# A recurrent attention block with dense layers on one core: the output projection with its weight as the stationary side, dense layers on rows of both network layers at once, and a lag of 4 steps instead of 6

## The chip, the core and the metric

The kernel runs on one core of a Trainium2 chip. The time is device microseconds of that core, as the median of several executions. The engines are called PE (TensorE), DVE (VectorE), ACT (ScalarE), POOL (GpSimd) and SP (the engine that only issues transfers here). The time before is 1830.54 us (3 runs, 1828.23 to 1834.61).

## The reference, cut to what matters

Two network layers with the same weights run one after the other. Each is an attention part that walks over the 2048 rows in 64 segments of 32 rows, then a dense part. The attention of a segment sees 8 memory rows and its 32 rows. The first 8 rows of its projected output are the memory of the next segment, so the 64 steps of one layer are a chain.

```python
def _A_ref(x, mem0, Wq, Wk, Wv, Wo, seg_len):        # 32 heads of 128, Dm = 512
    mem = mem0
    for s in range(n_seg):                            # 64 segments of 32 rows
        h = jnp.concatenate([mem, x[:, s*32:(s+1)*32, :]], axis=1)   # 40 rows
        q, k, v = (jnp.einsum('btd,dhe->bhte', h, W) for W in (Wq, Wk, Wv))
        p = _softmax(jnp.where(mask, q @ k^T * scale, -1e9))
        o = jnp.einsum('bhte,hed->btd', p @ v, Wo)
        mem = o[:, :M, :]                             # the chain
        outs.append(o[:, M:, :])
    return jnp.concatenate(outs, axis=1)
# ... cut: _B_ref(x) = relu(x @ w1) @ w2, with 1376 hidden columns
x = x + _A_ref(_layernorm(x), ...);  x = x + _B_ref(_layernorm(x), ...)
x = x + _A_ref(_layernorm(x), ...);  x = x + _B_ref(_layernorm(x), ...)
```

## The kernel before

The kernel works on both network layers in one step: layer one on segment k, layer two on segment k - DELTA (DELTA is the lag, 6). So there are 64 + 6 = 70 steps: 58 with both layers, and 6 with one layer at each end. The instruction order on each engine is found on the host before compilation, by a planner that tries 60 orders, partly at random from a seed, with assumed costs and keeps the best; its constants are no measurements. The order that it chose is then fixed: each engine executes its own queue in that order.

The projection has the attention's output as its stationary side (64 columns: 16 rows and both memories of layer one and two, and 32 rows of layer two) and Wo as the moving side (512 columns). Its result has rows on partitions. The next step's queries need the memory with the 512 features on partitions. So the memory is copied out, turned by small matmuls, and copied again: this is called the hand-over below.

```python
    def project(k, act, seg):
        ...
        for p in range(4):
            def mm(p=p):
                for hh in range(4):
                    for u in range(2):
                        h = 8 * p + 4 * u + hh
                        nc.tensor.matmul(wo[64 * u:64 * u + 64, :], lhsT=OT[:, h, HS:2 * L], rhs=Wo_sb[:, h, :],
                                         start=(p == 0 and hh == 0), stop=(p == 3 and hh == 3),
                                         tile_position=(0, 64 * u))
        ...                      # the hand-over:
            for half, eng in ((0, ACT), (1, DVE)):       # wm[:, half] <- wo[:, half], 128x256 each
                ...
            def tr(cols):                                # turn: mt <- wm against selm
                ...
            def ev():                                    # HTn memory columns <- mt (DVE)
                ...
        for a in act:                                    # row adds: x rows += wo, two per layer (DVE)
            ...
                plan.op(DVE, t_dve(512), add, r=[wo, x], w=[("x", g, c)])
        if 0 in act:                                     # OXb <- first 16 rows of layer one (POOL)
            ...

    def project_late(g):         # once in four steps: those 16 rows of four segments, 32 matmuls of 512
        ...                      # columns, a copy, a spread against selx, one add
```

The other 16 rows of each layer-one segment do not fit into the 64 columns; they wait for `project_late`. The dense part (`finish_group`) runs per layer on 128 rows, the rows of four segments. The values of each step are needed in a second place for layer one: transfers from on-chip memory to on-chip memory put them there (`place_values`: one transfer per half, which waits for all four value copies).

Of the kernel before, what the change touches and what calls it, by code (L numbers as in the profile page):

```python
# [18 lines left out]
DELTA = 6  # L19
# [9 lines left out]
PASSES = 60  # L29

# [53 lines left out]
class Op:  # L84
    __slots__ = ("eng", "cost", "fn", "preds", "succs", "bufs", "new", "given", "ready", "start", "end", "wait",
                 "after", "seq", "tile", "lag", "mode", "more")


class Plan:
# [7 lines left out]
    def op(self, eng, cost, fn, r=(), w=(), tile=WHOLE, lag=None, more=0.0):  # L97
        o = Op()
        o.eng, o.cost, o.fn, o.succs, o.seq, o.tile = eng, cost, fn, [], len(self.ops), tile
# [28 lines left out]
    def forward(self, prio, look, stay):  # L128
# [3 lines left out]

        for pool in self.pools:
            pool.reset()
# [6 lines left out]
        for o in self.ops:  # L141
            if not o.wait:
                cand[o.eng].append(o)
        count, tile = 0, WHOLE
        while count < len(self.ops):
            best = None
            for e in range(5):
                lo = None
                for o in cand[e]:
                    t = max(o.ready, free[e])  # L150
                    for pool, bufs in o.new:
                        t = max(t, pool.when(bufs))
                    o.start = t
                    if lo is None or t < lo:
                        lo = t
                if lo is not None and lo < 1e9 and (best is None or lo < best[0]):
                    best = (lo, e)
            assert best is not None, "no operation can be planned"
            lo, e = best
            o = min((c for c in cand[e] if c.start <= lo + look),  # L160
                    key=lambda c: (prio[c.seq] - (stay if e == PE and c.tile in (tile, EITHER) else 0.0), c.seq))
# [20 lines left out]
            for s in o.succs:  # L182
                s.ready = max(s.ready, seen)
                s.wait -= 1
                if not s.wait:
                    cand[s.eng].append(s)
# [47 lines left out]
    def order(self):  # L234
# [13 lines left out]
        rnd, best, look, stay = Random(1), None, 0.05, 0.5  # L248
        for n in range(PASSES):
# [5 lines left out]
            if best is None or total < best[0]:  # L255
                best = (total, [(o.start, o.seq, o.mode) for o in self.ops], [(b, b.i) for b in self.bufs], look, stay)
                base = late
# [3 lines left out]
        for _, seq, mode in best[1]:  # L261
            self.ops[seq].mode = mode
        return [self.ops[seq] for _, seq, _ in sorted(best[1])]
# [3 lines left out]
def kernel(  # L267
# [35 lines left out]

# [3 lines left out]
    LK = (0, L - HS)  # L307
    plan = Plan()
# [17 lines left out]
    p_x = Pool([sb(f"xg{i}", [128, Dm], F32) for i in range(4)], True)  # L326
    p_b = ring("bf512", 1, [128, Dm])
    x0 = p_x.buf()
    xb0 = p_b.buf()
    xb0_t = p_b.tiles[0]  # L330
# [40 lines left out]

    selm = sb("selm", [128, 2 * M])
    selx = sb("selx", [128, 128])

# [8 lines left out]
    def make_mask():  # L383
        nc.gpsimd.memset(maskb[:], 0.0)
        for g2 in range(2):
            blk = maskb[64 * g2:64 * g2 + SEG, 0, 0:HS]
            select(blk, ALU.is_ge, NEG, 0, -1, 1)
            select(blk, ALU.is_ge, NEG, HS - 1, 0, -1)
            blk = maskb[64 * g2:64 * g2 + SEG, 0, HS:SEG]
            select(blk, ALU.is_ge, NEG, -HS, -1, 1)  # L390
            select(blk, ALU.is_ge, 0.0, -HS, 0, 1)
# [3 lines left out]

    def make_selm():
        nc.gpsimd.memset(selm[:], 0.0)
        for u in range(2):
            select(selm[64 * u:64 * u + 64, :], ALU.not_equal, 1.0, -HS, -1, 1)

    def make_selx():
        nc.gpsimd.memset(selx[:], 0.0)
        for u in range(2):
            for c in range(GS):
                select(selx[64 * u:64 * u + 64, SEG * c + HS:SEG * (c + 1)], ALU.not_equal, 1.0, -HS * c, -1, 1)
# [11 lines left out]
    OXb = sb("OXb", [128, H, GS * HS])  # L417
    wxs = sb("wxs", [128, Dm])
    wm = sb("wm", [128, Dm])
# [7 lines left out]
    p_xn = [ring("xnA", 2, [128, NC4, 128], BF, True), ring("xnB", 1, [128, NC4, 128], BF, True)]  # L427
# [4 lines left out]
    def prepare():  # L432
# [10 lines left out]
        def zero_rest():  # L443
            nc.vector.memset(OT[:], 0.0)
            for t in (*Pt, *p_PT.tiles, V0, vw):
                nc.vector.memset(t[:], 0.0)

        def get_x():
            nc.scalar.dma_start(out=xb0_t[:], in_=A_x[0, 0:128, :])

        def get_memory():
            nc.scalar.dma_start(out=wm[0:M, :], in_=A_mem0[0, :, :])
# [3 lines left out]
        def turn():  # L456
            for c4 in range(NC4):
                nc.tensor.transpose(tp[:, :].bitcast(BF)[:, c4 * M:(c4 + 1) * M],
                                    wm[0:M, c4 * 128:(c4 + 1) * 128], ident[0:M, 0:M])
# [8 lines left out]
        columns = [("HTm", i) for i in range(2)] + [("HTx", i, a, c) for i in range(2) for a, c in ((0, 0), (0, HS), (1, X1))]  # L468
        plan.op(ACT, 0.45, get_x, w=[xb0])
        plan.op(ACT, 0.45, get_memory, w=[("wm", 0), ("wm", 1)])  # L470
# [3 lines left out]
        plan.op(DVE, 9.0, zero_rest, w=["zero PT"] + [("vw", p) for p in range(4)] + [("V0l", b) for b in range(2)] + [("OT", j) for j in range(8)] + [("P", p, b) for p in range(4) for b in range(2)])  # L474
        plan.op(POOL, 0.6, make_ident, w=["ident"])
        plan.op(POOL, 3.3, make_mask, w=["mask"])
        plan.op(POOL, 0.6, make_selm, w=["selm"])
        plan.op(POOL, 2.0, make_selx, w=["selx"])
        plan.op(PE, 0.2, turn, r=[("wm", 0), ("wm", 1), "ident", "memory"], w=[tp])
# [9 lines left out]
    def layernorm(x, rows, pool):  # L489

        ln, xn, xnT, tp = p_ln.buf(), p_b.buf(), pool.buf(), b_fill.buf()

        def stats():
            nc.vector.bn_stats(out=ln[:, 0:6], in_=x[:, :])

        def aggr():
            nc.vector.bn_aggr(out=ln[:, 6:8], in_=ln[:, 0:6])

        def eps():
            nc.vector.tensor_scalar_add(out=ln[:, 8:9], in0=ln[:, 7:8], scalar1=LN_EPS)  # L500

        def power():
            nc.gpsimd.tensor_tensor(out=ln[:, 8:9], in0=ln[:, 8:9], in1=mhalf_t[:], op=ALU.pow)

        def norm():
            nc.vector.tensor_scalar(out=xn[:, :], in0=x[:, :], scalar1=ln[:, 6:7], scalar2=ln[:, 8:9],
                                    op0=ALU.subtract, op1=ALU.mult)

        def turn(cols):
            for c4 in range(NC4):  # L510
                for u in range(0, 128, cols):
                    nc.tensor.transpose(tp[u:u + cols, :].bitcast(BF)[:, c4 * 128:(c4 + 1) * 128],
                                        xn[:, c4 * 128 + u:c4 * 128 + u + cols], ident[:], tile_position=(0, u))

        def keep():
            nc.scalar.copy(out=xnT[:, :, :].rearrange("p c t -> p (c t)"), in_=tp[:, :].bitcast(BF)[:, 0:512])
# [5 lines left out]
        plan.op(DVE, 0.50, norm, r=[x, ln, *rows], w=[xn])  # L522
        plan.op(PE, 0.23, turn, r=[xn, "ident"], w=[tp], tile=EITHER)
        plan.op(ACT, t_act(512), keep, r=[tp], w=[xnT])
        return xnT

    def dense_layer(x, rows):
        xnT = layernorm(x, rows, p_xm)
        hT = p_h.buf()
        for fb in range((NFC + 3) // 4):  # L530
# [14 lines left out]
            def relu(hp=hp, f0=fcs[0], n=nfull):  # L545
                nc.scalar.activation(out=hT[:, f0:f0 + n, :].rearrange("p f t -> p (f t)"), in_=hp[:, 0:n * 128],
                                     func=ACTF.Relu)

            def relu_last(hp=hp, n=nfull):
                nc.scalar.activation(out=hT[0:F_LAST, NFC - 1, :], in_=hp[0:F_LAST, n * 128:(n + 1) * 128],  # L550
                                     func=ACTF.Relu)

            plan.op(ACT, t_act(128 * nfull), relu, r=[hp], w=[hT, (hT, fb)])
            if nfull < len(fcs):
                plan.op(ACT, t_act(128), relu_last, r=[hp], w=[hT, (hT, fb)])
# [11 lines left out]
        def add():  # L567
            nc.vector.tensor_tensor(out=x[:, :], in0=x[:, :], in1=yp[:, :], op=ALU.add)

        plan.op(DVE, t_dve(512), add, r=[yp, x], w=rows)  # L570

    x_tiles, xnT_tiles = {}, {}

    def rows_of(g):
        return [("x", g, c) for c in range(GS)]

    def load_group(g):
        x, xb = (x0, xb0) if g == 0 else (p_x.buf(), p_b.buf())
# [4 lines left out]
        def widen():  # L583
            nc.vector.tensor_copy(out=x[:, :], in_=xb[:, :])

        if g > 0:
            plan.op(SP, 0.6, load, r=["loaded"], w=[xb, x])
        plan.available(xb0, 3.5)
        plan.op(DVE, 0.36, widen, r=[xb], w=[x, *rows_of(g)])
        x_tiles[g] = x  # L590
        xnT_tiles[(0, g)] = layernorm(x, rows_of(g), p_xn[0])

    def finish_group(a, g):
        x, rows = x_tiles[g], rows_of(g)
        dense_layer(x, rows)
        if a == 0:
            xnT_tiles[(1, g)] = layernorm(x, rows, p_xn[1])
            return
        assert out.dtype == BF
        ob = p_b.buf()  # L600

        def narrow():
            nc.scalar.copy(out=ob[:, :], in_=x[:, :])

        def store():
            nc.sync.dma_start(out=out[0, 128 * g:128 * (g + 1), :], in_=ob[:, :])

        plan.op(ACT, t_act(512), narrow, r=[x, *rows], w=[ob])
        plan.op(SP, 0.6, store, r=[ob])
# [13 lines left out]
    def t_copy(eng, n, rate=1):  # L623
        return t_act(n) if eng == ACT else t_dve(n, rate)

    def prep_x(k):
# [4 lines left out]
        for a in act:  # L631
            g, c = divmod(seg[a], GS)
# [383 lines left out]
```

## Time and profile before

| | before |
|---|---|
| median of 3 runs | 1830.54 us |
| profiled span | 1826.9 us |
| mean granted PE clock (share of full speed) | 0.986 |
| end of the first projection (start of its last matmul) | 58.5 us |
| a step with both layers (mean of 58) | 26.38 us |
| a step with one layer | 18 to 22 us |

The step times are differences between the starts of the last projection matmuls of successive steps, read from the trace.

First the page of the kernel before: the span, then busy time, share of the span and number of instructions of each engine (PEld is the weight load of a matmul), and the chain that ended last, by engine and by line.

```profile
span 1826.9 us, 84214 instructions
...
PE 1680.4 (92%) x37465; PEld 1293.2 (71%) x37465; DVE 1301.0 (71%) x3147; ACT 901.9 (49%) x2146; POOL 424.8 (23%) x1177
...
PE 75%; DVE 9%; DMA 7%; ACT 5%; issue 2%; SPq 1%; POOL 0%; POOLq 0%; ACTq 0%; DVEq 0%
```

The next view is the timeline of the kernel before around one hand-over; columns are start and duration in us, engine, line, operation, output<-inputs, shape, count and, in brackets, idle time of the engine before and what ended it.

```profile
923.67 1.06 PE L867 MATMUL st_123<-Wo_sb,OT 128*64 128x512 bf16 x8
...
924.53 1.06 PE L487 MATMUL fill_125<-w_sb,hT_117 128*64 128x512 bf16 x8
924.76 0.37 ACT L619 CAST wm<-st_123 128x256 bf16<-128x256 f32 x1 [1.44 <-PE st_123 L867]
925.16 0.43 DVE L621 CAST wm<-st_123 128x256 bf16<-128x256 f32 x1 [1.63 <-ACT wm L619]
...
925.39 0.48 PE L487 MATMUL work_122<-selm,wm 128*64 128x16 bf16 x8
925.62 0.68 DVE L906 TENSOR_TENSOR xg_68<-xg_68,st_123 16x512 f32<-16x512 f32 x1
...
926.33 0.23 DVE L890 CAST HT_79<-work_122 128x64 bf16<-128x64 f32 x1
926.39 1.03 PE L667 MATMUL fill_124<-Wv_sb,XG 128*64 128x512 bf16 x8
...
927.35 0.75 PE L719 MATMUL work_119<-HT_79,Wk_sb 128*128 128x80 bf16 x16
```

The last eight projection matmuls start at 923.67. ACT's copy, DVE's copy after it, the turn, a row add that got in between, and the memory copy into HT_79 take until 926.56. In the meantime PE runs dense matmuls and values of later rows (fill). The first query/key matmul starts at 927.35. On the mean of the both-layer steps, the last projection matmul starts 2.67 us before the next step's first query or key matmul, and the rest of the step (first query to last projection) takes 23.69 us.

Two groups of that hand-over from the table of groups (busy us, mean ns, idle before, releaser) show that DVE's half of the copy always follows ACT's (69 times of 69, 0.03 us after its end):

```profile
L621 DVE CAST wm<-st_123 128x256 bf16<-128x256 f32 x69 | 29.3, 425 | 105.9 <-ACT wm L619 105.9
L619 ACT CAST wm<-st_123 128x256 bf16<-128x256 f32 x69 | 25.7, 372 | 61.9 <-PE st_123 L867 61.9
```

The last view before the change is of the value tile V_87 in the stretch with both layers (241 to 1693 us): who waited for the transfers into it (us in all, times). PEld and PE together waited 41.1 us.

```profile
who waited for it (us, times):
  PEld L840: 10.8, 9
  PE work_120 L840: 9.3, 9
  PE work_118 L840: 9.1, 8
  PE work_121 L840: 4.5, 8
  PE work_122 L840: 3.8, 6
  PE work_119 L840: 3.6, 7
```

### The profile page before, as it was taken

To read this page: it belongs to the slowest core of one execution; us is meant where nothing else is said; L and a number is where in the kernel's file an instruction comes from. 1 tells how busy PE (TensorE), PEld (TensorE's weight loads), DVE (VectorE), ACT (ScalarE), POOL (GpSimd) and SP (SyncE) were. 2 spreads that over 40 slices of the span, in tenths; PEclk is the share of its full clock that TensorE was granted. 3 is DMA by queue.
4 is the path that set the end of the run, shared out by engine and by line. 5 is a ranking of instruction groups with operands and counts; after the bars stand their busy time and mean duration, and the time that the engine had idled before them with its cause. 6 is when DMAs were issued, how large, how long until landed. Compare 5 with 4: busy or idle time off the path is not lost.

```text
span 1826.9 us, 84214 instructions
## 1 busy us (share of the span) xinstructions
PE 1680.4 (92%) x37465; PEld 1293.2 (71%) x37465; DVE 1301.0 (71%) x3147; ACT 901.9 (49%) x2146; POOL 424.8 (23%) x1177
## 2 busy tenths in 40 slices
PE   3899999999999999999999999999999999999997
PEld 2666777776777777777776777777777777767775
DVE  3566677777777777777777777777777777677664
ACT  1344455545544554555555455545555455445443
POOL 3222222222222222222222122222222222122111
PEclk9899999999999999999999999999999999999999
DMA  9300000000000100000010000001000000000000
GB/s 358 106 19 16 14 18 21 17 19 17 14 19 17 23 14 19 17 18 20 13 24 14 19 17 17 20 13 23 17 18 15 20 17 18 16 17 17 3 6 5
DMA packets 22028, 50.17 MB, mean 27 GB/s; under 512 B 4408, under 2 KB 10560, under 8 KB 21664
## 3 DMA queue, kind: packets, MB, share of 16 engines
q1 hardware_dynamic: 18808, 34.52, 8.4%
q0 software_dynamic: 2560, 9.80, 1.4%
q8 instruction: 293, 4.80, 1.1%
q10 hardware_dynamic: 296, 0.47, 0.1%
q14 instruction: 71, 0.58, 0.1%
HBM read 21.70 MB, written 2.10 MB: 13 GB/s over the span
## 4 chain that ended last, share of the span: by engine, by line
PE 75%; DVE 9%; DMA 7%; ACT 5%; issue 2%; SPq 1%; POOL 0%; POOLq 0%; ACTq 0%; DVEq 0%
PE st_123 L867 11%; PE fill_125 L667 7%; PE fill_124 L667 7%; PE work_119 L719 7%; PE work_121 L719 7%; PE work_120 L719 7%; PE work_122 L719 7%; PE work_118 L719 6%; DMA V_87<-vw 5%; PE fill_125 L487 4%; PE fill_124 L487 3%; DMA Wq_sb<-in_A_Wq_dram 2%; DVE OT L621 1%; ACT vw L619 1%; PE fill_124 L925 1%
## 5 line engine op out<-in xcount | busy, mean ns | idle before, releaser
L719 PEld LDWEIGHTS <-Wk_sb 128*128 128x128 bf16 x8960 | 342.7, 100 | 41.7 <-issue 25.1
L719 PEld LDWEIGHTS <-Wq_sb 128*128 128x128 bf16 x8960 | 345.5, 100 | 20.4 <-DMA Wq_sb<-in_A_Wq_dram 13.3
L867 PE MATMUL st_123<-Wo_sb,OT 128*64 128x512 bf16 x2240 | 294.9, 384 | 7.7 <-ACT OT L619 6.6
L802 POOL TENSOR_TENSOR P_81<-es_100,sm_107 128x160 bf16<-128x160 f32 (+1 forms) x140 | 59.9, 449 | 721.5 <-DVE sm_107 L786 354.4
L867 PEld LDWEIGHTS <-OT 128*64 128x64 bf16 x2240 | 121.4, 111 | 72.9 <-ACT OT L619 11.4
L840 PEld LDWEIGHTS <-V_87 128*64 128x64 bf16 (+1 forms) x2044 | 91.0, 112 | 88.6 <-issue 65.4
L913 POOL COPY OXb<-OT 128x128 bf16<-128x128 bf16 x256 | 83.9, 328 | 199.0 <-DVE OT L621 126.2
L780 ACT ACTIVATE es_100<-es_100 128x320 f32<-128x320 f32 (+1 forms) x140 | 62.7, 448 | 117.5 <-DVE es_100 L774 116.0
L621 DVE CAST wm<-st_123 128x256 bf16<-128x256 f32 x69 | 29.3, 425 | 105.9 <-ACT wm L619 105.9
L487 PEld LDWEIGHTS <-w_sb 128*64 128x64 bf16 (+2 forms) x2432 | 88.8, 111 | 9.1 <-issue 1.0
L840 PEld LDWEIGHTS <-vw 128*64 128x64 bf16 x2048 | 85.7, 112 | 9.7 <-issue 2.8
L802 POOL TENSOR_TENSOR P_82<-es_101,sm_108 128x160 bf16<-128x160 f32 (+1 forms) x140 | 61.2, 458 | 102.5 <-DVE sm_108 L786 50.4
L667 PEld LDWEIGHTS <-HT_78 128*64 128x64 bf16 x1120 | 55.6, 110 | 40.9 <-issue 1.4
L667 PEld LDWEIGHTS <-HT_79 128*64 128x64 bf16 x1120 | 53.8, 109 | 35.7
L667 PE MATMUL fill_125<-Wv_sb,HT_78 128*64 128x512 bf16 x592 | 77.6, 384 | 0.6 <-ACT vw L619 0.5
L802 POOL TENSOR_TENSOR P_84<-es_101,sm_110 128x160 bf16<-128x160 f32 (+1 forms) x140 | 57.7, 434 | 80.2 <-DVE sm_110 L786 45.9
L802 POOL TENSOR_TENSOR P_83<-es_100,sm_109 128x160 bf16<-128x160 f32 (+1 forms) x140 | 57.7, 433 | 70.9 <-DVE sm_109 L786 41.0
L667 PE MATMUL fill_125<-Wv_sb,HT_79 128*64 128x512 bf16 x560 | 72.8, 382 | 0.0
L667 PE MATMUL fill_124<-Wv_sb,HT_79 128*64 128x512 bf16 x560 | 72.8, 381 | 0.0
L780 ACT ACTIVATE es_101<-es_101 128x320 f32<-128x320 f32 (+1 forms) x140 | 62.6, 447 | 17.1 <-DVE es_101 L774 14.8
L774 DVE TENSOR_TENSOR es_100<-es_100,mx_105 128x320 f32<-128x320 f32 (+1 forms) x140 | 67.6, 483 | 2.4
L667 PE MATMUL fill_124<-Wv_sb,HT_78 128*64 128x512 bf16 x528 | 68.8, 382 | 0.0
(373 smaller groups left out, 4345.8 us busy)
## 6 DMA issues: line engine op xcount, KB each, us to landing
V_87<-vw SPq DMA_DIRECT2D x126, 96.0 KB
V_87<-vg SPq DMA_DIRECT2D x126, 64.0 KB
Wq_sb<-in_A_Wq_dram SPq DMA_DIRECT2D x4, 1024.0 KB
Wk_sb<-in_A_Wk_dram POOLq DMA_DIRECT2D x4, 1024.0 KB, 15.2
Wv_sb<-in_A_Wv_dram SPq DMA_DIRECT2D x2, 1024.0 KB
Wv_sb<-in_A_Wv_dram POOLq DMA_DIRECT2D x2, 1024.0 KB, 17.4
Wo_sb<-in_A_Wo_dram POOLq DMA_DIRECT2D x2, 1024.0 KB, 29.8
Wo_sb<-in_A_Wo_dram SPq DMA_DIRECT2D x2, 1024.0 KB
```

Of the source, the lines that this page charges most:

```text
L487: nc.tensor.matmul(out_[u:v, :], lhsT=lhsT[:, u:v], rhs=rhs, start=start, stop=stop, tile_position=(0, u))
L619: nc.scalar.copy(out=out_, in_=in_)
L621: nc.vector.tensor_copy(out=out_, in_=in_)
L667: nc.tensor.matmul(vp[64 * b:64 * b + 64, :], lhsT=cols[:, c4, :], rhs=Wv_sb[:, c4, n * 512:(n + 1) * 512], start=(c4 == 0), stop=(c4 == N ...
L719: nc.tensor.matmul(qp[:, hi * 2 * L:hi * 2 * L + n], lhsT=W_sb[:, c4, h * Dh:(h + 1) * Dh], rhs=HT[:, c4, c0:c1], start=(c4 == 0), stop=(c ...
L774: nc.vector.tensor_tensor(out=es3(), in0=es3(), in1=mx[:, 4 * a_lo:4 * a_hi].unsqueeze(2).to_broadcast([128, 4 * na, L]), op=ALU.subtract)
L780: nc.scalar.activation(out=e, in_=e, func=ACTF.Exp, scale=SCALE)
L802: nc.gpsimd.tensor_tensor(out=o, in0=e, in1=s.unsqueeze(3).to_broadcast([128, na, 2, L]), op=ALU.mult)
L840: nc.tensor.matmul(o[u:u + cols, :, a, :], lhsT=V[:, p, hh * Dh + u:hh * Dh + u + cols], rhs=PT[:, a, hh, :, :], start=True, stop=True, ti ...
L867: nc.tensor.matmul(wo[64 * u:64 * u + 64, :], lhsT=OT[:, h, HS:2 * L], rhs=Wo_sb[:, h, :], start=(p == 0 and hh == 0), stop=(p == 3 and hh ...
L913: nc.gpsimd.tensor_copy(out=OXb[:, 8 * p:8 * p + 8, HS * c:HS * (c + 1)], in_=OT[:, 8 * p:8 * p + 8, 0:HS])
L925: nc.tensor.matmul(wl[64 * u:64 * u + 64, :], lhsT=OXb[:, h, :], rhs=Wo_sb[:, h, :], start=(t == 0), stop=(t == H // 2 - 1), tile_position ...
```

## The change

Its intent: Wo as the stationary side gives the projected output with the features on partitions, so the memory goes into the next step by one copy, and all rows are projected at once (no late projection). The rows are turned later, off the chain. The dense part takes 64 rows of each network layer at once, every two steps, and this allows a lag of 4 steps (68 steps: 60 with both layers, 8 with one).

```diff
-DELTA = 6
+DELTA = 4
@@ project @@
-                for hh in range(4):
-                    for u in range(2):
-                        h = 8 * p + 4 * u + hh
-                        nc.tensor.matmul(wo[64 * u:64 * u + 64, :], lhsT=OT[:, h, HS:2 * L], rhs=Wo_sb[:, h, :], ...)
+                for h in range(8 * p, 8 * p + 8):
+                    for c4 in range(NC4):
+                        nc.tensor.matmul(wo[:, 2 * W * c4 + c0:2 * W * c4 + c1], lhsT=Wo_sb[:, h, c4 * 128:(c4 + 1) * 128],
+                                         rhs=OT[:, h, c0:c1], start=(h == 0 and c4 == 0), stop=(h == H - 1), ...)
@@ hand-over: wm copies, turn and mt removed @@
+                nc.vector.tensor_copy(out=HTn[:, :, m_lo:m_hi], in_=v(2 * W)[:, :, m_lo:m_hi])
@@ row adds, OXb copies and project_late removed; rows are kept for the pair @@
+                copy_on(eng, ox[...][:, :, a0:a1, SEG * u:SEG * (u + 1)], v(2 * W)[...][:, :, a0:a1, 0:SEG])
@@ finish_group(a, g) becomes finish_pair(j), every second step: turn ox, add, dense layer on 64 + 64 rows @@
-            if c == GS - 1:
-                finish_group(a, g)
+        if k % 2 and k // 2 < NP + D2:
+            finish_pair(k // 2)
@@ copies out of PSUM: the planner chooses the engine @@
+    def copy_op(n, fn, r, w):
+        plan.op((ACT, DVE), (t_act(n), t_dve(n)), fn, r=r, w=w)
@@ place_values: two half-size transfers, each after two value copies, also in step 0 on ACT's queue @@
-            def dma(b=b, q=q):
-                q.dma_start(out=V0[64 * b + HS:64 * b + L, :, :], in_=vw[64 * b:64 * b + L - HS, :, :])
+        for p in range(0, 4, 2):
+            for b in range(2):
+                ...
+                plan.op(eng, 0.78, dma, r=[(name, p), (name, p + 1)], w=[("V0", late, p // 2, b)], lag=2.45)
```

Cut: planner support for the choice of engine, layer norm on part of the partitions, masks and buffers.

## The prediction

> **What bounds the kernel now.** TensorE. The busy table gives PE 92%, DVE 71%, ACT 49%, POOL 23%; the chain of waits is 75% PE. From the timeline, start-to-start spacing of matmuls: query/key (128x128 weights, 80 columns) 36 ns, with 40 columns 25; 128x64 weights with 512 columns 108 (old projection 116); 128x64 with 80 columns 21. The Trainium skill ("TensorE: Matmul & The Clock Gate", section "Back-to-back issue gap") says N/2.4 + 2.5 ns, with a floor near 25; the trace agrees. At median spacing the 37,465 matmuls need 1606 us of 1827. The rest: about 50 at the start (weights arrive; the first projection ends at 58.5) and the end, about 170 of waits and mode changes between. A step with both layers takes 26.4 us, 24.0 of it spacing; a step with one layer 18 to 22.
>
> **PE work, per both-layer step** (counts from the two built programs, spacing from this trace):
> - removed: projection 3.71, turn of the memory 0.22, late projection and its spread 0.94: 4.87 us;
> - added: 128 projection matmuls x 36 ns = 4.61 us; 0.12 us for turning projected and extra normalised rows;
> - dense matmuls about the same (34 passes of 128 rows for 32).
>
> The swap is nearly neutral. More attention runs on the whole array; mode changes fall from 460 to 408. Over the program 1567 us for 1606. Most of the 38 is the shorter lag: 68 steps for 70, with 8 single-layer steps for 12 and 60 both-layer steps for 58.
>
> **Waits.** The old hand-over after each projection: ACT copies half (0.37), then DVE the other half (0.43; the waits show DVE waiting for ACT's copy, 105.9 us in all), often a 0.68 row add between, the transposes, a 0.22 copy; then queries start. The new one is a single 0.22 copy. PE waits beside memory turn and spread are 0.38 + 0.24 us per step. I expect half of it to stay, since the scores-softmax-attention-projection chain remains and there is less independent work (late projection) to hide it: 2.4 us of waits per step become about 1.9. DVE loses four 0.68 us row adds per step (175 us in all), POOL 84 us of copies; both are off the critical path, so this shortens chains and is not itself time.
>
> **Sum.** Start 58 + 3 single steps x 20 = 118; 60 x 25.6 = 1536; 4 closing steps x 18 = 72; end 18: 1744. From spacing instead: 1567 + ends 50 + waits 130 to 165 = 1747 to 1782. I predict **1755 us**, 8 in 10 between **1722 and 1792**. Chances: faster by over 2% 0.90, within 2% 0.09, slower 0.01.
>
> **What would show each step right or wrong.** Projection spacing 36 ns; about 3,000 more matmuls; no group for late projection, memory turn or spread; idle of PE before a step's first query matmul, released by the DVE memory copy, at most 0.7 us; both-layer step 25.2 to 26.0 us; DVE busy near 1050 us.
>
> **What would make it wrong.** (a) The loads of Wo do not hide behind 80-column matmuls: spacing 45 ns would add 70 us. (b) With less filler the attention chain is laid bare: waits stay at 2.4 or more, total near 1785. (c) A lag of 4 leaves two steps for dense layer and normalisation, as before, but if layer two's rows come late, every second step stalls. (d) The half-size value transfers land after the attention wants them. (e) If chains were the true limit, waits could fall to 1 us per step: near 1700.

## The result and the profile after

The changed kernel takes 1722.84 us (median of 4 runs, 1722.66 to 1724.25) against 1832.44 us of the kernel before in the same rounds. The ratio is 0.9406, 95% interval 0.9386 to 0.9426. Ratios here are the mean time of one kernel's runs over that of the other's of the same rounds, so not quite the ratio of the medians. Results are correct.

The page of the changed kernel:

```profile
span 1722.5 us, 89836 instructions
...
PE 1632.0 (95%) x40536; PEld 1402.1 (81%) x40536; DVE 909.6 (53%) x2294; ACT 1096.3 (64%) x2657; POOL 357.8 (21%) x873
...
PE 86%; DVE 4%; ACT 3%; SPq 2%; POOL 1%; DMA 1%; issue 1%; ACTq 0%; POOLq 0%; DVEq 0%
```

The timeline of the changed kernel around one hand-over:

```profile
928.72 1.31 PE L876 MATMUL st_124<-OT,Wo_sb 128*128 128x80 bf16 x32
...
929.96 1.05 PE L684 MATMUL fill_125<-Wv_sb,XG 128*64 128x512 bf16 x8
930.07 0.23 DVE L892 CAST HT_79<-st_124 128x64 bf16<-128x64 f32 x1 [1.12 <-PE st_124 L876]
930.33 0.37 ACT L640 CAST OX_91<-st_124 128x256 bf16<-128x256 f32 x1 [1.03 <-DVE HT_79 L892]
...
930.95 0.43 PE L732 MATMUL work_121<-HT_79,Wq_sb 128*128 128x80 bf16 x7
```

The memory copy is over at 930.30, and the first query matmul starts at 930.95, behind one piece of filler. The rows' copy (OX_91) comes after it and is off the chain. In the table of groups the projection and the memory copy are:

```profile
L876 PE MATMUL st_124<-OT,Wo_sb 128*128 128x80 bf16 (+1 forms) x8704 | 345.7, 200 | 0.7 <-ACT OT L640 0.6
...
L892 DVE CAST HT_80<-st_124 128x64 bf16<-128x64 f32 (+1 forms) x34 | 7.5, 221 | 63.0 <-PE st_124 L876 63.0
```

The view of the value tile V_88 in the changed kernel, 153 to 1634 us, ends with no reader that waited for a transfer:

```profile
L708 SPq DMA_DIRECT2D V_88<-vw x236: 713/747/1672, 165.5 to 1626.1; - x118
...
who waited for it (us, times):
busy tenths in 40 slices 0001133233213322331332233133223313313300
```

To compare PE in all kernels, each matmul is given the spacing that its shape has when matmuls follow each other undisturbed in the trace (36 ns for 128x128 weights with 80 columns, 108 for 128x64 with 512, 21 for 128x64 with 80, and so on). Their sum in a step is "work"; the rest of the step is "waits" (waiting, mode changes and first-matmul gaps together). The last two columns cut a step at its two ends: last projection matmul to the next step's first query or key matmul, and from there to the last projection matmul.

| kernel | median us | both-layer step | work | waits | last projection to first query | first query to last projection |
|---|---|---|---|---|---|---|
| before | 1832.44 | 26.38 | 23.71 | 2.66 | 2.67 | 23.69 |
| after | 1722.84 | 25.09 | 23.71 | 1.41 | 0.82 | 24.28 |

Work and waits leave out a few steps at the ends, so they add up only to within 0.03. How the smallest shapes are weighed matters a little: a recount with other spacings for them gave 23.4 and 23.5 of work. So matmul work per step changed by little or nothing. The step became shorter by 1.29 us because the hand-over lost 1.85; the rest of the step gained 0.59, while it now holds 1.15 us more projection matmuls.

The spans differ by 104.4 us. The start is 9.9 us later (first projection ends at 68.4, not 58.5), the rest falls to the steps and to their number; the first experiment divides it.

The clock changed as well. The clock record of each trace shows windows of 3.4 us in which PE was granted half its speed (from 584.0 to 587.4 us of the kernel before, the granted clock is 0.50). In the both-layer stretch there are 8 such windows before and none after: a mean granted clock of 0.991 and 1.000. Among like steps of the kernel before (every fourth), the 7 with a window took 27.83 us and the 8 without 26.57. So the windows cost about 1.3 us each, some 10 us of the gain; this is an estimate from these two means. They came in kernels with more waits: none in the five that wait 1.39 to 1.84 us per step (tables here and below), 4 to 13 in those that wait 2.19 us or more. No run shows what sets them off.

### The profile page after: what moved, and what is told of

The parts are those of the page before. It is cut to its first block, busy times and chain, and to the rows that moved or that the text cites. A ratio compares the mean times of both kernels' runs of the same rounds, so it can differ in the third digit from the quotient of the medians.

```text
span 1722.5 us, 89836 instructions
## 1 busy us (share of the span) xinstructions
PE 1632.0 (95%) x40536; PEld 1402.1 (81%) x40536; DVE 909.6 (53%) x2294; ACT 1096.3 (64%) x2657; POOL 357.8 (21%) x873
## 4 chain that ended last, share of the span: by engine, by line
PE 86%; DVE 4%; ACT 3%; SPq 2%; POOL 1%; DMA 1%; issue 1%; ACTq 0%; POOLq 0%; DVEq 0%
PE st_124 L876 15%; PE fill_125 L684 8%; PE fill_126 L684 7%; PE work_122 L732 7%; PE work_120 L732 7%; PE work_123 L732 7%; PE work_119 L732 7%; PE work_121 L732 7%; PE fill_125 L481 6%; PE fill_126 L481 4%; SPq L365 1%; SPq L368 1%; POOL P_85 L814 1%; DMA w_sb<-in_B_w_dram 1%; PE work_119 L759 1%
## 5 line engine op out<-in xcount | busy, mean ns | idle before, releaser
L732 PEld LDWEIGHTS <-Wq_sb 128*128 128x128 bf16 x8704 | 336.0, 100 | 32.8 <-issue 19.1
L876 PE MATMUL st_124<-OT,Wo_sb 128*128 128x80 bf16 (+1 forms) x8704 | 345.7, 200 | 0.7 <-ACT OT L640 0.6
L876 PEld LDWEIGHTS <-Wo_sb 128*128 128x128 bf16 x8704 | 319.1, 100 | 10.8 <-issue 6.8
L640 ACT CAST vw<-fill_125 128x512 bf16<-128x512 f32 x134 | 78.0, 582 | 61.8 <-PE fill_125 L684 61.7
L640 ACT CAST vw<-fill_126 128x512 bf16<-128x512 f32 x132 | 76.9, 583 | 49.3 <-PE fill_126 L684 49.2
L481 PEld LDWEIGHTS <-w_sb 128*128 128x128 bf16 (+2 forms) x1752 | 89.7, 104 | 5.3 <-issue 4.8
L814 POOL TENSOR_TENSOR P_84<-es_100,sm_109 128x160 bf16<-128x160 f32 (+1 forms) x136 | 61.8, 476 | 135.8 <-DVE sm_109 L798 103.4
L773 DVE TENSOR_TENSOR es_100<-work_121,maskb 128x320 f32<-128x320 f32 (+1 forms) x38 | 18.5, 487 | 133.7 <-PE work_121 L759 133.7
L849 PEld LDWEIGHTS <-vw 128*64 128x64 bf16 (+1 forms) x1480 | 82.1, 106 | 5.6 <-issue 1.9
L481 PE MATMUL fill_125<-w_sb,hT_118 128*64 128x512 bf16 (+1 forms) x645 | 85.8, 380 | 0.0
L773 DVE TENSOR_TENSOR es_100<-work_119,maskb 128x320 f32<-128x320 f32 (+1 forms) x37 | 17.4, 469 | 122.3 <-PE work_119 L759 118.1
L792 ACT ACTIVATE es_100<-es_100 128x320 f32<-128x320 f32 (+1 forms) x136 | 61.9, 455 | 24.6 <-DVE es_100 L786 22.4
L684 PE MATMUL fill_125<-Wv_sb,HT_79 128*64 128x512 bf16 x560 | 72.9, 382 | 0.2 <-ACT vg L640 0.2
L684 PE MATMUL fill_126<-Wv_sb,HT_80 128*64 128x512 bf16 x560 | 72.3, 380 | 0.0
L684 PE MATMUL fill_125<-Wv_sb,HT_80 128*64 128x512 bf16 x528 | 68.2, 380 | 0.0
```

Source lines behind the costliest of these rows:

```text
L481: nc.tensor.matmul(out_[u:v, :], lhsT=lhsT[:, u:v], rhs=rhs, start=start, stop=stop, tile_position=(0, u))
L640: nc.scalar.copy(out=out_, in_=in_)
L684: nc.tensor.matmul(vp[64 * b:64 * b + 64, :], lhsT=cols[:, c4, :], rhs=Wv_sb[:, c4, n * 512:(n + 1) * 512], start=(c4 == 0), stop=(c4 == N ...
L732: nc.tensor.matmul(qp[:, hi * 2 * L:hi * 2 * L + n], lhsT=W_sb[:, c4, h * Dh:(h + 1) * Dh], rhs=HT[:, c4, c0:c1], start=(c4 == 0), stop=(c ...
L773: nc.vector.tensor_tensor(out=esv(), in0=spv(), op=ALU.add, in1=maskb[:, a_lo:a_hi, :].unsqueeze(2).to_broadcast([128, na, 4, L]))
L792: nc.scalar.activation(out=e, in_=e, func=ACTF.Exp, scale=SCALE)
```

## The experiments

Twelve kernels ran, each for three rounds beside the kernel before (medians 1825.49 to 1828.19 us in those rounds). All passed the comparison with the reference, even the two that leave out part of the result: presumably the projected rows that these omit are small beside x with these inputs, so the comparison does not see them. The table repeats the columns from above.

| kernel | median us | ratio to before | both-layer step | work | waits | last projection to first query | first query to last projection |
|---|---|---|---|---|---|---|---|
| after, lag 6 | 1754.47 | 0.959 | 25.16 | 23.65 | 1.52 | 0.92 | 24.26 |
| after, other seed | 1738.46 | 0.9504 | 25.29 | 23.69 | 1.61 | 0.96 | 24.32 |
| after, engines tied | 1752.44 | 0.958 | 25.54 | 23.72 | 1.84 | 1.05 | 24.51 |
| after, hand-over put back | 1784.68 | 0.9775 | 26.00 | 23.80 | 2.19 | 1.92 | 24.08 |
| after, hand-over off the chain | 1732.92 | 0.9495 | 25.25 | 23.87 | 1.39 | 1.08 | 24.17 |
| before, other seed | 1825.36 | 0.9997 | 26.32 | 23.71 | 2.60 | 2.66 | 23.64 |
| before, no late projection | 1824.65 | 1.0001 | 26.30 | 22.70 | 3.60 | 2.41 | 23.87 |
| before, short row adds | 1810.42 | 0.9916 | 26.11 | 23.70 | 2.39 | 2.34 | 23.73 |
| before, free engines | 1836.21 | 1.0055 | 26.54 | 23.78 | 2.75 | 2.51 | 23.99 |

Two theories stood against each other. "Hand-over": the step is as long as its chain, and the change took links out of it. "VectorE's queue": the vanished row adds and the free choice of engine let DVE serve PE sooner. In the texts below, DVE's 21.5 us per step is a sum of durations; counted without overlap, it was busy 1060.57 us in 54 steps of the kernel before, 19.6 us per step. The planner made a new order for every kernel below, so each difference also holds the luck of one order.

### The lag back at 6 (after_lag6)

```diff
-DELTA = 4
+DELTA = 6
```

> The changed kernel with the lag back at 6 steps (70 steps: 12 with one layer, 58 with both). If the lag is worth what the step times of the changed kernel say (two more single-layer pairs at 18 to 19 us, two fewer both-layer steps at 25.1), the time is 1722.8 + 4 x 18.6 - 2 x 25.1 = about 1747 us, and a both-layer step stays at 25.1. Rival: the lag of 4 also makes the steps themselves tighter or looser (less or more slack for the dense layers); then the both-layer step moves by more than 0.2 us and the time leaves 1740 to 1755.

Measured: 1754.47 us, 31.6 more than the changed kernel (1754.47 - 1722.84). The both-layer step hardly moved (25.16 for 25.09, 4 us over 58 steps); the other 27 us are the four more single-layer steps less two both-layer steps. So the lag is worth about 30 us. Against the kernel before, which has the same 70 steps, this kernel's span is 73.5 us shorter: 58 x (26.38 - 25.16) = 71 us in both-layer steps, about 13 in the ends, less 10 for the late start.

### Another planner seed (after_seed2, before_seed2)

```diff
-SEED = 1        # in the kernel before: Random(1) becomes Random(2)
+SEED = 2
```

> The changed kernel with another seed of its instruction planner, nothing else: how far the luck of the order goes. If the gain comes from the change, the time stays within 10 us of 1722.8. If much of it is a lucky order, it is 20 us or more away.

> The kernel before with another seed of its planner: how far the luck of the order goes there. The changed kernel moved by 16 us. If it is alike, 1828 plus or minus 20, and the 15 us of the cut row adds and the 11 us of the free engine choice are within it.

Measured: the changed kernel at 1738.46 us, 15.6 slower than with seed 1; the kernel before at 1825.36 us, the same (ratio 0.9997). So the choice of order can be worth 16 us in the changed kernel, and a difference of that size from one order is no evidence. The gain as a whole is far outside it.

### The start: whole transfers in step 0 (after_head)

In the changed kernel, ACT issues eight value transfers in step 0. The timeline of ACT alone shows them standing in the way of its copies (ACTq is ACT's sequencer, here issuing transfers):

```profile
30.12 9.85 ACTq L708 DMA_DIRECT2D V_88<-vw  x2
40.01 0.29 ACT L640 CAST qT_92<-work_121 128x160 bf16<-128x160 f32 x1 [13.06 <-DMA Wv_sb<-in_A_Wv_dram]
...
54.94 4.03 ACTq L708 DMA_DIRECT2D V_88<-vg  x2
```

The bracket names a weight transfer as what ended ACT's wait. But the matmuls whose results these copies read were over by 32.4 us; from then on only the issues stood before the copies in ACT's queue.

```diff
-        for p in range(0, 4, 2):
+        wide = 4 if k == 0 else 2
+        for p in range(0, 4, wide):
```

> The changed kernel, but in step 0 alone the value transfers are issued whole (4 instead of 8 on ScalarE's queue). Theory: the changed kernel's first step ends 10 us later (68.4 us against 58.5) because those transfer issues hold up ScalarE's queue for 9.9 and 4.0 us while the weights load; then the first step ends near 59 and the time is 1712 to 1716 us. Rival: the first step is late because of the weights themselves or the larger zeroing; then the first step still ends after 65 and the time stays at 1720 or more.

Measured: 1714.99 us, ratio 0.9376. The first projection ends at 61.6 us. The same view of this kernel has four issues, none of them long:

```profile
44.25 1.26 ACTq L709 DMA_DIRECT2D V<-vg  x2
46.61 1.60 ACTq L709 DMA_DIRECT2D V<-vw  x2
49.13 0.29 ACT L640 CAST qT<-work 128x160 bf16<-128x160 f32 x1 [2.95 <-PE work L734]
```

So the splitting had cost the start 6.8 of the 9.9 us. Whole transfers wait for all four value copies, so they are also issued later (44.25 us instead of 30.12, when more of the weights have landed); their number and their moment changed together. The other 3.1 us stay open. All other steps kept their times (both-layer step 25.09), so this difference, though small, is not the planner's luck in the steps. This is the fastest kernel.

### Engines tied down (after_fixed) and freed in the kernel before (before_flex)

```diff
-        plan.op((ACT, DVE), (t_act(n), t_dve(n)), fn, r=r, w=w)
+        plan.op(e, t_act(n) if e == ACT else t_dve(n), lambda: fn(e), r=r, w=w)    # e: as in the kernel before
```

> The changed kernel with each PSUM copy tied to ScalarE or VectorE as in the kernel before (new copies on ScalarE), instead of the planner's choice. If the free choice of engine is a main cause of the shorter waits, the time rises by 20 us or more. If the hand-over and the vanished row adds are, it stays within 10 us.

```diff
-            eng = (ACT, DVE)[x]                        # and so for each copy out of PSUM in the kernel before
-            plan.op(eng, t_copy(eng, 4 * na * L), ev, r=[pv[x]], w=[("OT", 2 * p + x)])
+            copy_op(4 * na * L, ev, r=[pv[x]], w=[("OT", 2 * p + x)])
```

> The kernel before with the planner of the changed kernel, so that each PSUM copy goes to ScalarE or VectorE as the plan finds best; nothing else. In the changed kernel tying the copies down cost 0.45 us per both-layer step (30 us in all). If the free choice gains the same by itself, this is near 1800 us; since VectorE is busier here, theory 'VectorE's queue' expects 1785 to 1800 and VectorE's busy time per step down from 21.5 to under 19 us. Theory 'hand-over' expects 1815 or more, as the two copies of the memory still follow one another.

Measured: tied copies cost the changed kernel 29.6 us (1752.44), above the 16 us of luck but not far above. Free copies made the kernel before a little slower (1836.21, ratio 1.0055), although DVE's sum per step fell from 21.5 to 18.2 us. Relief for DVE alone bought nothing there. What the free choice is worth depends on the rest of the kernel; it is not a gain that can be added up.

### Short row adds in the kernel before (before_noadd)

```diff
-                    rows = x[SEG * c:SEG * c + n, :]
+                    rows = x[SEG * c:SEG * c + n, 0:8]          # wrong result on purpose
```

> The kernel before with its four row adds per step cut to 8 of 512 columns (wrong result on purpose; same order of dependences). In it VectorE is busy 21.5 us of each 26.4 us step; this takes 2.3 us of that away and nothing from TensorE. Theory 'VectorE's queue': the long adds delay the copies that TensorE waits for, so waits fall by 0.4 us a step or more and the time is 1803 us or less. Theory 'hand-over': only the chain projection, two copies, turn, copy matters; then the time stays above 1815. Another planner order alone moved the changed kernel by 16 us, so between the two nothing is settled.

The planner's cost of the adds was cut too. Measured: 1810.42 us, 15 less (ratio 0.9916). That is between the two expectations and the size of the planner's luck in the other kernel, so it settles little; if all of it is real, it is a fifth of the 73.5 us. Half-clock windows fell from 8 to 4, which at 1.3 us each is about 5 of the 15 us.

### The hand-over put back (after_handover), and beside the chain (after_offchain)

```diff
-            def ev():
-                nc.vector.tensor_copy(out=HTn[:, :, m_lo:m_hi], in_=v(2 * W)[:, :, m_lo:m_hi])
+            for half, eng in ((0, ACT), (1, DVE)):
+                ...      # wm[:, two chunks] <- wo[:, two chunks]
+            def tr(cols):
+                for c4 in range(NC4):
+                    across(cols, mt[:, c4 * 2 * M:(c4 + 1) * 2 * M], ident[:], wm[:, c4, SEG:SEG + 2 * M])
+            def ev():
+                nc.vector.tensor_copy(out=HTn[:, :, m_lo:m_hi], in_=mt[...])
```

> The changed kernel with the old hand-over of the memory put back behind the new projection: half copied by ScalarE, half by VectorE, eight small matmuls against the identity, then the copy into the next step's columns (right result). Theory 'hand-over': PE waits rise by 0.4 us a step or more, the time is 1748 us or more. Theory 'VectorE's queue': the added chain is covered by other matmuls; the time stays below 1735, little more than the 0.2 us of added matmuls and the planner's luck (16 us).

The control executes the same instructions, but the last copy goes to a tile that nobody reads, and the direct copy feeds the next step:

```diff
-                nc.vector.tensor_copy(out=HTn[:, :, m_lo:m_hi], in_=mt[...])
+                nc.vector.tensor_copy(out=wn[:, :, ...], in_=mt[...])
+            def direct():
+                nc.vector.tensor_copy(out=HTn[:, :, m_lo:m_hi], in_=v(2 * W)[:, :, m_lo:m_hi])
```

> The control of the last hand-over run: the same two copies, eight small matmuls and last copy are executed after each projection, but into a tile that nobody reads, while the next step takes its memory from the single direct copy (right result). If it is the length of the chain that cost 62 us, this stays within 20 us of the changed kernel (1722.8). If it is the added instructions on PE, ScalarE and VectorE, it is as slow as the put-back hand-over, 1765 us or more.

Measured: 1784.68 us with the old hand-over in the chain, 61.8 more than the changed kernel; 1732.92 us with the same instructions beside the chain, 10.1 more, of which 0.16 us x 60 = 10 is their matmul work. So about 52 us come with the length of the chain and not with the added instructions. Two things limit that figure: each kernel has one planner order (another order moved the changed kernel by 16 us), and the put-back kernel has 8 half-clock windows in its both-layer stretch where the control has none. At half speed for 3.4 us, 8 windows cost at most 14 us, so most of the 52 us is left. Last projection to first query went from 0.82 to 1.92 us in the one and to 1.08 in the other.

The wait itself is mostly seen elsewhere. PE's waits in the both-layer stretch of the kernel with the hand-over put back (engine, line, waited for: us in all, times, longest):

```profile
PE work L851 <- ACT PT L642: 34.7, 31, 1.9
PE work L483 <- ACT wm L642: 5.7, 15, 0.4
...
PE work L483 <- DVE wm L644: 2.5, 15, 0.2
```

and in its control:

```profile
PE work L852 <- ACT PT L643: 19.7, 33, 0.9
...
PE work L484 <- ACT wm L643: 3.4, 12, 0.3
```

The added wait for the turned memory is only a few us; the wait for the softmax result (PT) grew by 15. The reading that fits, not tested by itself: work that could wait (filler) was moved into the longer hand-over, and was then missing while PE waits for PT. A longer chain then shows up where the filler has run out, not at the link that was added.

### The late projection taken away from the kernel before (before_nolate)

```diff
-        if 0 in seg and seg[0] % GS == GS - 1:
-            project_late(seg[0] // GS)                 # wrong result on purpose
```

> The kernel before without the late projection, its spread and its add (wrong result on purpose). It takes away 16 times 3.46 + 0.22 us of matmuls, 59 us, and the waits beside the spread, 14 us. If TensorE's work sets the pace everywhere, the time falls by 55 to 75 us, to 1753 to 1773. If the late projection mostly fills gaps in which PE would wait for the chain anyway, it falls by less than 35 us.

Measured: 1824.65 us, ratio 1.0001 (0.9981 to 1.0021). About 59 us of matmuls vanished, and the time did not move. Per step, work fell by 1.01 us and waits rose by 0.94. In a stretch of equal length, 54 steps of the kernel before, PE's busy time (after the stretch and its length, with the number of matmuls) fell from 1344 to 1316 us; that is less than the work fell, as overlapping matmuls are counted once. Before:

```profile
267.40:1693.00 1425.60, 1344.04 (x29904) 1043.26 (x29902) 1060.57 (x2446) 733.19 (x1672) 339.89 (x909) 0.99 0.09 18
```

and without the late projection:

```profile
267.40:1693.00 1425.60, 1315.90 (x29366) 1036.88 (x29365) 1061.68 (x2440) 723.22 (x1662) 329.68 (x906) 0.99 0.09 18
```

So the kernel before, with PE 92% busy, was not limited by the amount of PE's work. Its late projection ran in time that PE would otherwise have spent waiting. (The planner made a new order for this kernel; that a better order could have used the freed time is not excluded.) The clock is a rival, but a small one: this kernel has 13 half-clock windows in its both-layer stretch, the kernel before 8. Five more cost at most 5 x 1.7 = 8.5 us, far less than 59, and the steps without a window take the same in both, 26.12 and 26.14 us.

### Other lags (before_lag5, after_head_lag3)

```diff
-DELTA = 6
+DELTA = 5        # the kernel before; groups of four segments do not allow 4
```

> The kernel before with a lag of 5 steps (4 is not possible there: layer two's rows come from a group of four steps that ends one step too late). 69 steps, 10 with one layer. If the lag's worth is only the step count, the time falls by 2 x 19.5 - 26.4 = 13 us, to about 1815. If the group's dense layers then come late for layer two, both-layer steps grow by 0.3 us or more on average and the time is not below 1828.

```diff
-DELTA = 4
+DELTA = 3        # the changed kernel with whole transfers in step 0; the last pair is finished after the loop
```

> The changed kernel with whole value transfers in step 0 and a lag of 3 steps: 67 steps, 6 with one layer, 61 with both. It leaves one step instead of two between a pair's last projection and the first use of its rows by layer two. If one step is slack enough, the time falls by 2 x 19 - 25.1 = 13 us to about 1702. If the dense layers come late then, every second step stalls: both-layer steps over 25.5 us and a time of 1725 or more.

Measured: the kernel before with lag 5 takes 1881.17 us (ratio 1.0308), slower by 3% although it has a step less. Nearly every fourth step takes 30 to 31 us instead of 26. These long steps hold about 27.9 us of matmul work against 20.7 to 22.6 in the other three, and PE idles 1.0 us in them against 2.3 to 3.0. So PE is not kept waiting in the long steps; dense work falls into one step and is missing as filler in the others. The changed kernel with lag 3 takes 1727.43 us (ratio 0.946), 12 more than with lag 4, with step times of about 23.9, 26.6, 23.7 and 27.6 in turn; PE waits for the copied rows of a pair before it turns them, 18.5 us in 30 waits or 0.30 per step. Both-layer steps average 25.41, just under the 25.5 that the expectation gave to the stall, and 12 us is within the planner's luck, so only this is shown: lag 3 gave no gain. For the kernel before, a shorter lag was a loss; the changed kernel, with its pairs, bears a lag of 4.

## Why the prediction was right or wrong

**The time: right, but only just, and by luck.** 1722.84 us lies at the very bottom of 1722 to 1792. The predicted gain was 75.5 us (1830.5 - 1755); the measured one is 110 (1832.4 - 1722.8). Two errors of opposite sign kept it in the range: the steps were shorter than foretold (60 x (25.6 - 25.09) = 31 us) and the start was 9.9 us longer. With most of the start mended (after_head, 1714.99) the time lies below the range.

**"What bounds the kernel now. TensorE": wrong.** Busy shares and the chain of waits were taken as proof. Removing 59 us of matmuls (before_nolate) gave nothing. The both-layer step behaved like a loop of memory, query, softmax, projection and hand-over: lengthening one link lengthened the step (after_handover). The chain of waits shows 75% PE all the same; our reading is that PE executes its queue in the planned order, so that the chain runs through whatever filler stands in the queue. The prediction's own point (e), chains as the true limit and a time near 1700, was nearer than its main line.

**"The swap is nearly neutral": right in size, wrong in weight.** Projection matmuls with 80 columns are 36 ns apart, as predicted, and there are 3071 more matmuls; work per both-layer step is 23.71 us in both kernels. But neutrality of PE's work was not the question.

**"I expect half of it to stay ... 2.4 us of waits per step become about 1.9": this is the step that failed.** In the units of the tables above, waits went from 2.66 to 1.41, a fall of 1.25 instead of 0.5. The estimate looked at PE's idle time beside the hand-over and the spread (0.62 us) and took off 0.5 for "half of it". The hand-over's length was the right quantity: 2.67 us before, 0.82 after. Putting it back cost 62 us, of which 10 are its instructions and at most 14 the half-clock windows that came with it. It also feared that less filler would lay the chain bare; no harm of less filler is seen once the chain was shorter.

**The lag: right.** The prediction put most of 38 us on it; going back to 6 cost 31.6.

**The start: missed, with the sign against the change.** "Start 58" was 68.4. The split transfers on ACT's queue account for 6.8 of the 9.9 us. Point (d) of the prediction looked for late transfers in the steps and did not look at the issuing queue in step 0.

**The engines: DVE near 1050 was 910**, and ACT, for which the prediction gave no figure, rose from 902 to 1096 us, because the planner moved copies from DVE to ACT. The counts in the two built programs would have told it. "Off the critical path" for the row adds is not refuted: short row adds gained 15 us at one order. "First query idle at most 0.7 us" held (the longest wait of a query matmul for the memory copy is 0.3 us), but could hardly fail: in the kernel before it was 0.7 us. The both-layer step of 25.09 is just under the 25.2 to 26.0 foretold.

**What stays open.** Of 71 us in both-layer steps at an equal number of steps, about 50 answer to the hand-over (52 us in 60 steps), if the figure from the changed kernel holds there too. About 10 of the 71 us come through the half-clock windows, which that share overlaps. The rest is not divided: tied engines cost 30 us in one kernel and freed ones gained nothing in the other. The 41.1 us that PE waited for value transfers before, and 0 after, suggest that the half-size transfers help in the steps while they hurt in step 0; no run separates this. Waits that look separate here are not additive, as filler moves between them. And the changed kernel is no longer bound by its chain everywhere: in every second both-layer step (mean 24.5 us) PE idles less than 0.05 us by the profile, so a shorter chain alone could hardly gain anything there; in the other steps (25.6 us) it idles 0.6 to 1.9 us.

## What to carry to other kernels

In a recurrent loop, find the chain from one step's result to the next step's first use and measure its length in the trace, before counting the busy engine's work: 92% busy is no proof of a limit when part of the work is filler, and taking a piece of filler away on purpose is a cheap test. Choose operand sides so that the result leaves the matmul in the layout in which the next step reads it, even at about three times as many matmuls (8704 for 2752 here). When one order out of many is fixed by a planner, run a second seed before believing any difference of one per cent.

## What the Trainium skill lacked or had wrong

- "TensorE: Matmul & The Clock Gate", section "Back-to-back issue gap": its formula N/2.4 + 2.5 ns, called there the gap of an isolated matmul, is what this case's trace shows also when every matmul has its own new 128x128 weights: 36 ns at 80 columns, 25 ns at 40 (the section's floor), 56 ns at 128 (dense layer). The section's sustained figure for such pairs, about 81 ns at 128 columns, is not seen here.
- "Trainium Kernel Development and Optimization", section "Performance Expectations", names the weight-load busy share, beside MFU (the share of peak arithmetic that is reached), as a good metric for how near a kernel is to its roofline. Here it was 71% before and 81% after. The page does not say that the share cannot tell whether PE's work or a chain sets the time: with 71%, 59 us of matmuls could be removed from the kernel before with no change of time. "Perfetto Trace Analysis", section "Optimization Strategy", says to find the gaps on the engine and what blocks it; it does not say that in a loop the gap may appear elsewhere than at the link that is too long (34.7 us of waits for PT, and 5.7 and 2.5 for the links that were put back).
- "TensorEngine Tiling (Array Packing)", section "Key Properties", says that a change of tiling mode drains the engine, without a size. Here both-layer steps have 6.96 changes before and 6.04 after; time beyond the plain spacing at them is 0.98 and 0.69 us per step, 0.14 and 0.11 us each (waits that fall on a change included).
- No page tells how long the issue of a transfer on a compute engine's queue can take while large transfers are in flight; it would belong to "DMA: Bandwidth & Descriptors". Here two issues took 9.85 us on ACT while the weights were loading, and ACT's next copy stood behind them; in the kernel with whole transfers two issues took 1.26 us.
